# Three PSUM banks as three tiles, and as one tile only while the scores of two heads hold them

## The chip, the cores and the metric

The kernel runs on 1 core of one Trainium2 chip. The metric is device time in microseconds (us), the median of the runs. TensorE (PE) multiplies matrices; its products go to PSUM, which this kernel uses as eight banks of 128 partitions by 512 fp32 values, and VectorE (DVE) and ScalarE (ACT) read them there. GpSimd (POOL) does some of the work on SBUF, and SyncE (SP) issues the DMAs.

## The reference

An attention layer with a bias made by a small network, a feed-forward layer, and a layer of eight experts of which each token takes one. Cut to what matters:

```python
# attention: q, k, v are (2, 8, 576, 64)
scores = q @ k^T / sqrt(64) + bias        # bias: relu(x @ w1 + b1) @ w2, x from the positions
attn = exp(scores - max); attn /= sum(attn) + 1e-9
x = (attn @ v) as (1152, 512)
# feed-forward
h = x @ w_in                              # 512 -> 2048
g = h * tanh(log(1 + exp(h)))
x = g @ w_out                             # 2048 -> 512
# experts: each token to the expert of its largest logit, at most `capacity` tokens each
y = relu(x_e @ w1[e]) @ w2[e]
out[i] = gate[i] * y[expert of i, place of i]
```

## The kernel before, in words

The 1152 tokens are worked off in five tiles of rows (`NIT` = 4 tiles of 128 rows of both batches, and one of the rest). For each tile there are blocks of the bias (`bias_block`, L473 on PE, read out at L487 to L490), the attention (`pair` for the scores and the softmax, `recips`, `pv_pair`), the feed-forward layer (`mlp_a`, L726 on PE, read at L731 by ACT and at L283 by DVE; `mlp_b`, L759) and the choice of the expert (`y_out`, `rank_of`; L827, L843, L848, L907). Until about 460 us these parts are interleaved; after that the experts run one by one (L1182 to L1271).

Each of these steps is recorded with `op(...)`. The table `ORDER` says in which order the recorded steps are emitted and on which engine each runs. This order is fixed by hand ahead of the build, so each engine's queue is fixed, and an engine that waits at the head of its queue holds all that stands behind it. What an instruction waits for is not written in the kernel: the framework records, tile by tile, who wrote and read, and puts semaphore waits in front of an instruction that comes too soon.

PSUM is shared out by the ring `RB` of eight slots, one for a bank. Slots 3 to 7 (`pb0` to `pb4`) are five tiles of 512 columns. Slots 0 to 2 are slices of one tile, `ps`, of 3 x 512 columns:

```python
ps_ = psp.tile([P, 3, 512], F32, name="ps")
RB = Ring([ps_[:, i] for i in range(3)] + [psp.tile([P, 512], F32, name=f"pb{i}") for i in range(5)], {(0, 1, 2): ps_.rearrange("p a b -> p (a b)")})
```

`pair` takes the slots 0 to 2 together, since the scores of two heads fill 1536 columns: four products of 512 columns (L535; each counts twice in the trace, since fp32 goes in two passes) and a last piece (L538). DVE reads the two heads in turn (L552). At other times each of the three slots is taken alone, for a product of `mlp_a` (L726), a block of the bias (L473), three transposes (L561, copied to SBUF at L564), or small products (L599, L848, L907). `Ring.take` picks the free slot that was given back longest ago, and the three only when nothing else is free. The names `ps` and `pb` in the trace tell which tile an instruction writes or reads; which third of `ps` it is the trace does not tell.

Of the kernel before, what the change touches and what calls it, by code (L numbers as in the profile page):

```python
# [9 lines left out]
F32 = mybir.dt.float32  # L10
# [9 lines left out]
PSUM = bass.MemoryType.PSUM  # L20
DRAM = bass.MemoryType.DRAM

P = 128
# [119 lines left out]
class Buf:  # L143
    def __init__(self, ring, spans):
        self.ring, self.spans, self.left, self.slot = ring, spans, 0, None
# [6 lines left out]
class Ring:  # L152
# [12 lines left out]
    def take(self, b):  # L165
        def rank(x):
            whole = len(x) == 1 and any(x[0] in g and self.open(g) for g in self.groups)
            return whole, max(self.since[i] for i in x), x
        b.slot = min((x for x in b.spans if self.open(x)), key=rank)
        for i in b.slot:  # L170
            self.since[i] = None
# [4 lines left out]
            self.since[i] = self.clock  # L176


class Op:
    __slots__ = ("deps", "bufs", "allocs", "ways", "bytes", "late", "grp", "mode")  # L180


class Plan:
# [9 lines left out]
    def op(self, eng, ns, fn, r=(), w=(), p=(), bytes=0, alt=(), hold=(), lk=None, late=0.0, grp=None, mode=0):  # L193
        o = Op()
        o.ways = [(eng, ns, fn, eng == "POOL" if lk is None else bool(lk))] + [x if len(x) > 3 else x + (x[0] == "POOL",) for x in alt]
        o.late, o.bytes, o.grp, o.mode = late, bytes, grp, mode
        o.deps, o.bufs, o.allocs = set(), [], []
        for x in r:
            assert self.wr.get(x), ("read before any write", x)
            o.deps.update(self.wr[x])  # L200
            self.rd.setdefault(x, []).append(o)
        for x in list(w) + list(p):
            o.deps.update(self.rd.get(x, ()))
            if isinstance(x, Buf) and (x in p or not self.wr.get(x)):
                o.allocs.append(x)
        for x in w:
            o.deps.update(self.wr.get(x, ()))
            self.wr[x], self.rd[x] = [o], []
        for x in p:
            if self.rd.get(x):  # L210
                o.deps.update(self.wr.get(x, ()))
                self.wr[x], self.rd[x] = [o], []
            else:
                self.wr.setdefault(x, []).append(o)
        o.deps.discard(o)
        for x in {id(x): x for x in list(r) + list(w) + list(p) if isinstance(x, Buf)}.values():
            x.left += 1
            o.bufs.append(x)
        for x in hold:
            x.left += 1  # L220
            o.bufs.append(x)
        self.ops.append(o)
        return o
# [40 lines left out]
def tile_kernel(ctx: ExitStack, tc: tile.TileContext, a: dict, cap: int):  # L264
# [9 lines left out]
    def pool_of(stack, name, side="left", space=None):  # L274
        args = dict(name=name, bufs=1)
        args.update(dict(space=space) if space is not None else dict(side=side))
        return stack.enter_context(tc.tile_pool(**args))
# [35 lines left out]
    psp = pool_of(ph1, "psp", space=PSUM)  # L313
# [26 lines left out]
    def ring(p, name, n, shape, dt):  # L340
        return Ring([p.tile(shape, dt, name=f"{name}{i}") for i in range(n)])
# [9 lines left out]
    RX = Ring([PX[:, 2048 * i:2048 * i + 2048].rearrange("p (a b c) -> p a b c", a=2, b=4) for i in (1, 0)])  # L351
    RM = ring(p1, "rm", 12, [P, 2], F32)
    RSM = ring(p1, "rsm", 3, [P, 8], F32)
    ps_ = psp.tile([P, 3, 512], F32, name="ps")
    RB = Ring([ps_[:, i] for i in range(3)] + [psp.tile([P, 512], F32, name=f"pb{i}") for i in range(5)], {(0, 1, 2): ps_.rearrange("p a b -> p (a b)")})
    LONG = range(3, 8)


# [52 lines left out]
    def over_partitions(col, r):  # L411


        ps = pl.buf(RB)
        op("PE", 300, lambda: pe.matmul(ps.t[:, 0:P], col.to_broadcast([P, P]), ident, start=True, stop=True), bytes=0.5, r=r + ["ident"], w=[ps])
# [27 lines left out]
    def bias_const():  # L443
        cps = pl.buf(RB)

        def f():
            for c in range(4):
                pe.matmul(cps.t[32 * c:32 * c + 32, 0:1], w2s, b1c, start=True, stop=True)
        op("PE", 150, f, bytes=0.5, r=["w2s", "b1"], w=[cps], mode=3)
        op("ACT", c_act(1), lambda: act.copy(cb, cps.t[:, 0:1]), r=[cps], w=["cb"])  # L450
# [3 lines left out]
    def bias_block(blk):  # L454
# [12 lines left out]
        for d0 in range(0, dn, 512):  # L467
            d1 = min(dn, d0 + 512)
            ps = pl.buf(RB)

# [53 lines left out]
    def pair(it, ct, b):  # L524
        s_ = pl.buf(RB, group=True)
        q_ = qs[it]
# [29 lines left out]
        for n in range(3):  # L556
            pa = pl.buf(RB)

# [19 lines left out]
    def recips(it, ct):  # L578
        sm, n = sums[it, ct], 2 if it < NIT else 1

        rb[it, ct] = b_ = pl.buf(R2)
        rp = pl.buf(RB)
        wide = lambda: b_.t[:, 256:256 + P * n]
# [551 lines left out]
    man = tc.manual_schedule()  # L1135
    man.__enter__()
    pl.emit()
    ph1.close()


# [243 lines left out]
```

## Time and profile before

| what | value |
|---|---|
| time, median of 3 runs | 589.54 us (588.83 to 595.59) |
| the profiled execution's own time | 590.54 us |
| its span, first to last instruction | 588.8 us |
| busy on PE | 501.7 us (85%) |
| busy on DVE, ACT, POOL | 409.5, 355.5, 148.8 us |
| mean granted TensorE clock | 0.947 of full speed |

The span is counted from the first instruction to the last; the time of an execution has 1.7 us more around it. Busy time is an average over the whole span; a wait is read from the idle time of an engine just before an instruction, which the profile puts down to the instruction that ended last of those waited for.

### The profile page before, as it was taken

The page shows a single profiled execution, that of the slowest core. Times are in us where ns is not written, and L with a number is a line of the kernel's source. Part 1 is how long each engine was busy: PE and PEld are TensorE (multiplying, and loading weights), DVE is VectorE, ACT ScalarE, POOL GpSimd, SP SyncE. Part 2 cuts the span into 40 slices and gives each one's busy share as a digit, 9 for nine tenths or more (in the row PEclk, how much of TensorE's full clock was granted, in tenths as well). Part 3 has the DMA queues.
Part 4 walks back from the last instruction along what each step waited for, and adds up shares of the span by engine and source line. Part 5 has one row for each costly group of instructions (what it writes and reads, how often), then busy time and mean ns, then how long its engine had stood idle before and what let it go on. Part 6 is the DMA issues. An engine that isn't in the chain of part 4 may idle for free.

```text
span 588.8 us, 11288 instructions
## 1 busy us (share of the span) xinstructions
PE 501.7 (85%) x4212; PEld 353.1 (60%) x4212; DVE 409.5 (70%) x957; ACT 355.5 (60%) x718; POOL 148.8 (25%) x162
## 2 busy tenths in 40 slices
PE   1655788998979788999999999999899379999975
PEld 0211455675567453445578756689558369998963
DVE  5999999887856466786656774559878634746363
ACT  6999998775575586548864673326563134535351
POOL 3641424203102232301020432102523411131312
PEclk9876799999999998999999999999999669999998
DMA  7998866500102024242574000104105155181810
GB/s 295 382 344 265 294 226 195 204 1 1 41 1 89 15 81 124 80 143 77 178 203 150 0 1 3 38 1 164 72 2 180 19 189 178 51 303 60 299 42 29
DMA packets 28468, 73.92 MB, mean 126 GB/s; under 512 B 5126, under 2 KB 5254, under 8 KB 26352
## 3 DMA queue, kind: packets, MB, share of 16 engines
q1 hardware_dynamic: 26704, 68.95, 34.7%
q0 software_dynamic: 1696, 4.11, 2.2%
q8 instruction: 36, 0.59, 0.4%
q14 instruction: 32, 0.26, 0.2%
HBM read 55.67 MB, written 17.61 MB: 124 GB/s over the span
## 4 chain that ended last, share of the span: by engine, by line
PE 44%; DVE 22%; issue 15%; DMA 7%; ACT 7%; POOL 3%; SPq 0%; POOLq 0%; DVEq 0%; ACTq 0%
PE pb L759 9%; PE pb L726 8%; DMA xg<-yscr,gid 5%; PE ps L726 4%; PE ps L535 4%; PE pb L618 4%; DVE rw L283 4%; PE pb L561 3%; DVE ra L552 2%; DVE ra L280 2%; PE ps L561 2%; DVE WOt L283 2%; DMA w2b<-w 2%; PE ps L538 2%; PE pb L763 2%
## 5 line engine op out<-in xcount | busy, mean ns | idle before, releaser
L726 PEld LDWEIGHTS <-WIt 128*128 128x128 f16 x960 | 85.2, 98 | 25.9 <-issue 11.2
L726 PE MATMUL pb<-PX,WIt 128*128 128x256 f16 (+1 forms) x648 | 71.5, 265 | 2.7 <-DVE ra L283 2.0
L461 ACT ACTIVATE ra<-AT,b1c,stab 128x384 f32<-128x384 f32 (+13 forms) x74 | 51.8, 740 | 5.3 <-PE ps L473 2.2
L759 PE MATMUL pb<-WOt,ra 128*128 128x512 f16 x228 | 54.3, 383 | 0.2 <-POOL ra L741 0.2
L473 PE MATMUL pb<-ra,w2s 128*32 128x512 f32 (+15 forms) x246 | 39.5, 612 | 16.5 <-DVE rbe L490 5.3
L553 ACT ACTIVATE ra<-ra,rm 128x576 f32<-128x576 f32 x56 | 43.2, 774 | 10.2 <-DVE rm L552 9.9
L535 PE MATMUL ps<-AT,rq 64*128 64x512 f32 (+1 forms) x160 | 42.5, 662 | 8.0 <-DVE rm L552 6.6
L280 POOL TENSOR_SCALAR rw<-rw 128x1024 uint32<-128x1024 uint32 (+1 forms) x19 | 28.6, 1507 | 59.4 <-DMA rw<-wo 23.3
L552 DVE CUSTOM_DVE_ANT_0 ra<-ps,ra 128x576 f32<-128x576 f32 x50 | 36.4, 753 | 8.4 <-PE ps L538 3.9
L1215 PE MATMUL py<-HH,W 128*128 128x288 f32 x288 | 40.5, 298 | 0.0
L1014 DVE TENSOR_TENSOR W<-AT,W 128x1024 fp32r<-128x1024 f32 x28 | 33.7, 1224 | 9.6 <-ACT W L1013 8.9
L726 PE MATMUL ps<-PX,WIt 128*128 128x256 f16 (+1 forms) x312 | 31.7, 256 | 9.2 <-ACT ra L461 3.1
L1215 PEld LDWEIGHTS py<-HH,W 128*128 128x128 f32 x288 | 38.9, 188 | 0.0
L759 PE MATMUL pb<-WOt,rw 128*128 128x512 f16 x156 | 38.3, 387 | 0.0
L618 PE MATMUL pb<-ra,AT 128*64 128x128 f32 (+1 forms) x620 | 35.8, 266 | 0.9 <-DVE ra L632 0.9
L759 PEld LDWEIGHTS <-ra 128*128 128x128 f16 x228 | 21.8, 98 | 24.1 <-issue 1.5
L618 PEld LDWEIGHTS pb<-ra,AT 128*64 128x64 f32 x620 | 30.6, 137 | 5.1 <-issue 2.5
L283 DVE SCALAR_TENSOR_TENSOR rw<-rw 128x1024 int32<-128x1024 int32 (+1 forms) x26 | 31.8, 1226 | 0.1
L473 PEld LDWEIGHTS pb<-ra,w2s 128*32 128x32 f32 x246 | 10.1, 128 | 33.0 <-issue 8.6
L561 PE MATMUL pb<-ident,ra 128*128 128x128 f32 x180 | 28.6, 286 | 1.3 <-ACT ra L553 0.9
L1013 ACT ACTIVATE W<-AT 128x1024 fp32r<-128x1024 f32 x28 | 29.0, 1055 | 0.0
L538 PEld LDWEIGHTS ps<-AT,rq 128*128 128x128 f32 (+1 forms) x80 | 10.7, 183 | 29.0 <-issue 28.2
(395 smaller groups left out, 1101.5 us busy)
## 6 DMA issues: line engine op xcount, KB each, us to landing
AT<-m SPq DMA_DIRECT2D x32, 512.0 KB, 6.0
bscr<-rbe SPq DMA_DIRECT2D x36, 295.5 KB, 2.9
rw<-wo SPq DMA_DIRECT2D x8, 1024.0 KB, 5.0
ra<-bscr SPq DMA_DIRECT2D x28, 288.0 KB, 4.1
WOt<-wi SPq DMA_DIRECT2D x4, 1024.0 KB, 9.8
rw<-wi SPq DMA_DIRECT2D x4, 1024.0 KB, 9.1
AT<-k SPq DMA_DIRECT2D x4, 576.0 KB, 7.3
out<-ra SPq DMA_DIRECT2D x9, 256.0 KB, 6.0
```

Of the source, the lines that this page charges most:

```text
L280: eng.tensor_scalar(out=out, in0=in0, scalar1=s1, scalar2=s2, op0=op0, op1=op1)
L283: (eng or dve).scalar_tensor_tensor(out=out, in0=in0, scalar=s, in1=in1, op0=op0, op1=op1)
L461: on_act = lambda h_=h_, g=g: act.activation(h_.t[:, 0:dn], T[:, 0:dn], AF.Relu, scale=stab[:, g:g + 1], bias=b1c)
L473: pe.matmul(ps.t[32 * c:32 * c + 32, 0:d1 - d0], w2s, hs[c].t[:, d0:d1], start=True, stop=True)
L535: pe.matmul(s_.t[r, 1024 * i:1024 * i + 512], q_.t[hs, c], kraw[hs, k0 + 576 * bb:k0 + 576 * bb + 512], start=True, stop=True)
L552: op("DVE", c_dve(S), lambda i=i, own=own, m_=m_, b_=b_: dve.tensor_tensor_reduce(out=own(), in0=blk(s_.t[:, 960 * i:960 * i + S]), in1=bl ...
L553: op("ACT", c_act(S, 2), lambda i=i, m_=m_, col=col: act.activation(t_.t[:, S * i:S * i + S], t_.t[:, S * i:S * i + S], AF.Exp, bias=m_.t[ ...
L561: pe.transpose(pa.t[:, P * j:P * j + P], t_.t[:, 384 * n + P * j:384 * n + P * j + P], ident)
L618: pe.matmul(ov[64 * i:64 * i + 64, ct % 2, w * bb:w * bb + w], v_, t_.t[:, at + c0:at + c0 + w], start=n == 0, stop=n == 4)
L726: pe.matmul(ps.t[:, n * f_:n * f_ + n], WI[:, wv, ct, P * ft:P * ft + P], xt.t[:, xv, ct, 0:n], start=i == 0, stop=i == 11)
L759: pe.matmul(y_.t, gv()[:, g2, c:c + P], WO[:, wv, ft], **kw)
L1215: pe.matmul(ps[:, 0:SL], W2[:, wv, ft, P * dt:P * dt + P], HH[:, hv, ft], start=ft == 0 and i == 0, stop=ft == 7 and i == 2)
```

## The change

The ring `RB` becomes a `Banks`, which opens a pool of PSUM tiles for slots 0 to 2 whenever their use changes. While `pair` holds them, the pool has one tile of 1536 columns; while slots are taken singly it has three tiles of 512 columns. `take` closes the pool and opens the next when a slot below 3 is taken in the other manner than last time. `pb0` to `pb4` stay as they are. `ORDER`, the steps and the choice of slots are untouched.

```diff
+class Banks(Ring):
+
+
+    def __init__(self, tiles, get):
+        super().__init__([None] * 3 + tiles, {(0, 1, 2): None})
+        self.get, self.pool, self.whole, self.count = get, ExitStack(), None, 0
+
+    def take(self, b):
+        super().take(b)
+        if b.slot[0] < 3 and self.whole is not (len(b.slot) == 3):
+            self.pool.close()
+            self.whole, self.count = len(b.slot) == 3, self.count + 1
+            new = self.get(self.pool, f"pz{self.count}", 1 if self.whole else 3)
+            if self.whole:
+                self.groups[b.slot] = new[0]
+            else:
+                self.tiles[:3] = new
+
...
-    ps_ = psp.tile([P, 3, 512], F32, name="ps")
-    RB = Ring([ps_[:, i] for i in range(3)] + [psp.tile([P, 512], F32, name=f"pb{i}") for i in range(5)], {(0, 1, 2): ps_.rearrange("p a b -> p (a b)")})
+    RB = Banks([psp.tile([P, 512], F32, name=f"pb{i}") for i in range(5)], lambda st, name, n: [p.tile([P, 1536 // n], F32, name=f"ps{i}") for p in [pool_of(st, name, space=PSUM)] for i in range(n)])
...
     pl.emit()
+    RB.pool.close()
     ph1.close()
```

In the built program the five `pb` tiles lie in banks 0 to 4 and the shared three in banks 5 to 7 (before: `ps` in 0 to 2). The pool is opened 22 times, 11 times with one tile and 11 times with three. Every engine has the same instructions in the same order as before; lines from 461 on stand 18 lower in the changed file (L726 is L744 there). What differs is the names of the tiles and the waits. In the rows below, the word in brackets names the semaphore of the engine that an instruction waits for; the number behind a tile's name tells tiles apart.

The first place is on PE near 161 us: three transposes, a block of the bias and the first product of a step of `mlp_a`, which hold the three banks. `ps_140` is the one tile. Before:

```order
L561 MATMUL ps_140<-ident_82,ra4_115 128x128 [waits Activation_49]
L561 MATMUL ps_140<-ident_82,ra4_115 128x128 x2
L473 MATMUL ps_140<-ra1_112,w2s_94 32x320 [waits Activation_49]
L473 MATMUL ps_140<-ra0_111,w2s_94 32x320
L473 MATMUL ps_140<-ra6_117,w2s_94 32x320 x2
L726 LDWEIGHTS WIt_105
L726 MATMUL ps_140<-PX_107,WIt_105 128x256
```

The same place now:

```order
L579 MATMUL ps1_1395<-ident_82,ra4_115 128x128 [waits Activation_49]
L579 MATMUL ps1_1395<-ident_82,ra4_115 128x128 x2
L491 MATMUL ps2_1396<-ra1_112,w2s_94 32x320
L491 MATMUL ps2_1396<-ra0_111,w2s_94 32x320
L491 MATMUL ps2_1396<-ra6_117,w2s_94 32x320 x2
L744 LDWEIGHTS WIt_105
L744 MATMUL ps0_1394<-PX_107,WIt_105 128x256 [waits Activation_49]
```

The wait for ACT has gone from the block of the bias, and one for ACT stands four products later, ahead of the step of `mlp_a`, whose bank `ps0` ACT had read last.

The second place is on PE near 168 us: three transposes, the transposes of `recips` into a `pb` tile, and the next step of `mlp_a`. Before:

```order
L561 MATMUL ps_140<-ident_82,rw0_108 128x128 x3
L599 MATMUL pb0_141<-ident_82,ra9_120 128x128 [waits Activation_49]
L599 MATMUL pb0_141<-ident_82,ra9_120 128x128
L726 LDWEIGHTS WIt_105
L726 MATMUL ps_140<-PX_107,WIt_105 128x256 [waits Activation_49]
```

The same place now:

```order
L579 MATMUL ps2_1396<-ident_82,rw0_108 128x128 [waits Activation_49]
L579 MATMUL ps2_1396<-ident_82,rw0_108 128x128 x2
L617 MATMUL pb0_140<-ident_82,ra9_120 128x128 [waits Activation_49]
L617 MATMUL pb0_140<-ident_82,ra9_120 128x128
L744 LDWEIGHTS WIt_105
L744 MATMUL ps1_1395<-PX_107,WIt_105 128x256 [waits DVE_49]
```

The step of `mlp_a` waited for ACT, which had read the step before it out of another bank; now it waits for DVE, which copies the transposes out of this bank (`ps1`).

The third place is on PE near 200 us: the end of a block of the bias and the next step of `mlp_a`. Before:

```order
L473 MATMUL ps_140<-rw0_108,w2s_94 32x320
L473 MATMUL ps_140<-ra7_118,w2s_94 32x320 [waits DMAHW6_49]
L473 MATMUL ps_140<-rw1_109,w2s_94 32x320 [waits Activation_49]
L726 LDWEIGHTS WIt_105 [waits DVE_49]
L726 MATMUL ps_140<-PX_107,WIt_105 128x256 [waits Activation_49]
```

The same place now:

```order
L491 MATMUL ps1_1395<-rw0_108,w2s_94 32x320
L491 MATMUL ps1_1395<-ra7_118,w2s_94 32x320 [waits DMAHW6_49]
L491 MATMUL ps1_1395<-rw1_109,w2s_94 32x320 [waits Activation_49]
L744 LDWEIGHTS WIt_105
L744 MATMUL ps2_1396<-PX_107,WIt_105 128x256
```

The two waits ahead of the step of `mlp_a`, for DVE and for ACT, have gone, and none has come in their place.

## Rows read from the trace of the kernel before

**Rows 1.** The page's first part: each engine's busy time, share of the span, instructions.

```profile
PE 501.7 (85%) x4212; PEld 353.1 (60%) x4212; DVE 409.5 (70%) x957; ACT 355.5 (60%) x718; POOL 148.8 (25%) x162
```

**Rows 2.** Groups of PE, 160 to 440 us: busy, mean ns; idle before them, releasers.

```profile
L726 PE MATMUL pb<-PX,WIt 128*128 128x256 f16 (+1 forms) x511 | 55.2, 263 | 0.2 <-POOL PX L292 0.2
L726 PE MATMUL ps<-PX,WIt 128*128 128x256 f16 (+1 forms) x312 | 31.7, 256 | 9.2 <-ACT ra L461 3.1 <-DVE rw L283 2.0 <-ACT rw L731 1.7
...
L618 PE MATMUL pb<-rw,AT 128*64 128x128 f32 (+1 forms) x180 | 10.5, 265 | 0.6 <-DVE ra L632 0.6
...
L848 PE MATMUL ps<-sum,lg 128*128 128x8 f32 x2 | 0.4, 266 | 2.9 <-ACT rw L731 2.9
```

**Rows 3.** Timeline of PE: start, length, instructions; in brackets idle before, releaser.

```profile
161.62 0.74 PE L473 MATMUL ps<-ra,w2s 128*32 128x320 f32 x8 [0.57 <-ACT ra L564]
...
165.60 0.55 PE L561 MATMUL ps<-ident,rw 128*128 128x128 f32 x3 [1.17 <-ACT rbe L488]
...
169.69 0.93 PE L726 MATMUL ps<-PX,WIt 128*128 128x256 f16 x7 [1.68 <-ACT rw L731]
...
190.28 0.93 PE L726 MATMUL ps<-PX,WIt 128*128 128x256 f16 x7 [1.05 <-ACT rbe L487]
...
200.75 0.94 PE L726 MATMUL ps<-PX,WIt 128*128 128x256 f16 x7 [3.10 <-ACT ra L461]
...
213.72 1.03 PE L726 MATMUL ps<-PX,WIt 128*128 128x256 f16 x8 [0.55 <-ACT rbe L488]
...
222.35 0.39 PE L848 MATMUL ps<-sum,lg 128*128 128x8 f32 x2 [2.87 <-ACT rw L731]
...
246.39 0.58 PE L473 MATMUL ps<-ra,w2s 128*32 128x464 f32 x1 [0.72 <-DVE ra L564]
...
253.79 1.13 PE L535 MATMUL ps<-AT,rq 64*128 64x512 f32 x4 [1.31 <-ACT rbe L487]
...
348.32 0.52 PE L561 MATMUL ps<-ident,ra 128*128 128x128 f32 x3 [0.74 <-DVE ra L564]
...
372.28 0.33 PE L599 MATMUL ps<-ident,ra 128*128 128x128 f32 x1 [0.56 <-DVE ra L564]
...
385.15 0.93 PE L726 MATMUL ps<-PX,WIt 128*128 128x256 f16 x7 [0.82 <-ACT ra L731]
...
414.29 0.93 PE L726 MATMUL ps<-PX,WIt 128*128 128x256 f16 x7 [0.68 <-DVE rw L283]
...
426.02 0.96 PE L726 MATMUL ps<-PX,WIt 128*128 128x128 f16 x14 [1.30 <-DVE rw L283]
```

**Rows 4.** Timeline near the first three stalls and the seventh, of PE, ACT and DVE.

```profile
158.86 0.55 PE L561 MATMUL ps<-ident,ra 128*128 128x128 f32 x3
159.25 1.47 PE L726 MATMUL pb<-PX,WIt 128*128 128x256 f16 x12
160.56 0.49 PE L561 MATMUL ps<-ident,ra 128*128 128x128 f32 x3
...
161.08 0.48 ACT L564 COPY ra<-ps 128x384 f32<-128x384 f32 x1 [1.79 <-PE ps L561]
...
167.90 1.02 DVE L564 COPY rw<-ps 128x384 f32<-128x384 f32 x2 [2.41 <-PE ps L561]
...
218.91 0.27 ACT L846 COPY lg<-pb 128x128 f32<-128x128 f32 x1 [1.42 <-PE pb L843]
```

**Rows 5.** Busy time of each engine in two stretches, then granted clock, DMA share, GB/s.

```profile
220.00:222.30 2.30, 0.00 (x0) 0.00 (x0) 2.14 (x5) 2.30 (x6) 0.00 (x0) 1.00 0.00 0
222.30:225.00 2.70, 2.65 (x9) 1.14 (x10) 1.93 (x6) 0.75 (x3) 2.10 (x2) 0.65 0.63 231
```

**Rows 6.** Timeline of PE from 222 us: products of the same form.

```profile
222.60 2.23 PE L759 MATMUL pb<-WOt,ra 128*128 128x512 f16 x6
224.62 2.42 PE L759 MATMUL pb<-WOt,rw 128*128 128x512 f16 x6
...
227.84 1.46 PE L759 MATMUL pb<-WOt,ra 128*128 128x512 f16 x6
```

**Rows 7.** The page's costliest groups: DVE's read of one head's scores.

```profile
L552 DVE CUSTOM_DVE_ANT_0 ra<-ps,ra 128x576 f32<-128x576 f32 x50 | 36.4, 753 | 8.4 <-PE ps L538 3.9 <-issue 3.8 <-PE pb L618 0.6
```

## The prediction

> **What bounds the kernel now.** I read the busy times first. PE is busy for 501.7 of 588.8 us and no other engine for more than 70% [rows 1], so what shortens the kernel is work taken from PE or idle time taken out of its queue. The edit takes no product away; it can only act on waits. So I read, second, PE's groups by line for 160 to 440 us, where the three shared banks are most in use and all parts interleave. The reader is to see what stands behind the second bar, the idle time before a group. The steps of `mlp_a` that go to the five separate tiles (`pb`) have 0.2 us of it over 511 products; the 312 that go to the shared tile (`ps`) have 9.2 us. The largest other `pb` group has 0.6 us, while two small products into `ps` alone have 2.9 us [rows 2]. The same product, the same releasing engines, and yet the idle time lies with one tile.
>
> Third, I followed PE's timeline and noted each product into `ps` that came after more than half a microsecond of idle time. From 160 us on there are 14 [rows 3]. Their idle times are 0.57, 1.17, 1.68, 1.05, 3.10, 0.55, 2.87, 0.72, 1.31, 0.74, 0.56, 0.82, 0.68 and 1.30, which is 17.12 us. After each of them PE goes on at once, so that the end of the program hangs on them.
>
> **What kind of waits they are.** Take the first. Three transposes go into one third of `ps` and end at 159.41 (158.86 and 0.55). ACT is free, but its copy of them starts only at 161.08, when the next three transposes, which go to another third, have ended at 161.05 (160.56 and 0.49). Then PE's block of the bias, for the last third, waits for that copy to end at 161.56 [rows 3, 4]. Neither wait is for the data or for the bank; both follow from the three banks being one tile to whatever sets the waits. At 167.90 DVE shows the same: it had been idle for 2.41 us when its copy began, behind the last products into `ps` [rows 4]. The order of the two programs says that these waits are the ones that go: at the first place the block of the bias has lost its wait, at the third the step of `mlp_a` has lost both.
>
> [...]
>
> **The change, part by part.**
>
> *Waits that go outright.* Nine stalls wait for an instruction that read or wrote another third, or for something behind such an instruction, and what remains to be waited for ended before PE was free: 0.57, 1.05, 3.10, 0.55, 2.87, 0.72, 0.56, 0.82 and 1.30, together 11.54 us [rows 3]. For the one of 2.87 it can be read: the small product needs ACT's copy `lg`, which ended at 219.18 (218.91 and 0.27), while the wait was for a read of `ps` that ended just ahead of 222.35 [rows 3, 4].
>
> *Waits that stay, but for something that comes sooner.* Five products wait for a true reader of their own bank, and that reader was itself held by a false wait: 1.17, 1.68, 1.31, 0.74 and 0.68, together 5.58 us [rows 3]. The one of 1.68 is the second place in the order: the step of `mlp_a` will wait for DVE's two copies, which began at 167.90 after 2.41 us of idleness [rows 4]; begun when their transposes are done, they are out of PE's way. The scores at 253.79 (1.31) take all three banks and truly need the last block of the bias read out, but ACT came to that late for the same reason.
>
> What is late next? After a stall is gone PE runs on to the next product whose wait was satisfied before, so it meets the engines behind it at the same distances as now: ACT and DVE get their inputs earlier by the same amount, and at 60% and 70% busy [rows 1] they are not the queue that sets the pace. A wait that is satisfied just in time still costs the step from release to start: 161.56 to 161.62, 0.06 us [rows 3, 4]. I keep this for all 14: 17.12 − 14 × 0.06 = 16.3 us. Bounds: 11.54 − 9 × 0.06 = 11.0 us where only the nine go, and 17.1 where nothing is kept.
>
> [...]
>
> [...]
>
> *What is added.* The pool is opened 22 times. At an opening, the first product waits for all that used the three banks before, PE's own products among them. In the order some of these products wait for two engines where they waited for one. Nothing in the trace shows a wait of PE for itself; the nearest row is the step of 0.06 us for a wait that is just satisfied, so 22 × 0.06 = 1.3 us at most where such waits are long fulfilled, and 0 where they lie beside products still running. I take 0.6. The idle time that covers it is none: PE is the busy engine.
>
> [...]
>
> *What is not touched.* From 460 us on, the experts use other tiles and start from the end of what stands ahead of them, so they move forward as a whole.
>
> **The sum.** Against the profiled execution: 590.54 − 16.3 − 1.7 + 0.6 = 573.1 us. That execution was 1.0 us above the median of 589.54, so the median becomes 572.1 us.
>
> **The rivals.**
>
> *Only the outright waits go.* When PE is earlier, the true readers of each bank may not be: ACT and DVE have other work queued ahead (ACT's L461 fills its gaps), and then the five second-hand stalls stay and the clock may drop as before. 590.54 − 11.0 + 0.6 − 1.0 = 579.1 us, or 577.4 with the clock's 1.7. For it: ACT is the named releaser in nine of the 14. Against: its idle times beside them, as the 1.79 us ahead of the copy at 161.08 [rows 4], show that it was waiting too, not busy.
>
> *The stalls are a lack of banks, and nothing goes.* All eight banks are in use, and a product that finds none free must wait however the banks are named. The time would be 589.5 us. [...] Against it stand the 0.2 us of the `pb` groups, which share the same pressure [rows 2], and the waits that the order shows to have gone.
>
> *Openings cost more than the false waits.* At an opening, the new tiles can only be used when all readers of the old are done. Where a single bank was free after one head's read, it now waits for the second too, 0.75 us [rows 7]; at worst PE stands for both heads' reads, 1.5 us, at each of 22 openings. That is 33 us, and 590.54 − 16.3 + 33 − 1.0 = 606 us, slower by 2.8%. It decides from 18.0 / 22 = 0.82 us an opening. Against it: half of the openings are for the scores, which took all three banks before too, and in the other half the scores' readers are mostly long done, since slots 0 to 2 are taken singly only when nothing else is free.
>
> **How the numbers follow.** Forecast 0.75, only the outright waits 0.15, nothing goes 0.06, slower 0.04. The range reaches up to the first rival's 579.1 and, for the scatter of the runs shown (0.7 us from the median to the fastest), to 579.8; down to 590.54 − 17.1 − 1.7 − 0.8 − 1.0 = 569.9, where nothing is kept of the 14, openings cost nothing and the idle time before the two `pb` groups goes as well (0.2 and 0.6 [rows 2]), and 0.7 less, 569.2. Left out are the two last rivals and some of the ends. About 2%, 11.8 us, is what a measurement of this kernel tells from no change; the line is at 577.7. The forecast lies below it, and a third of the first rival: 0.80 faster, 0.17 within, 0.03 slower.
>
> **What the changed profile would show.** PE's idle time before products into `ps0` to `ps2` from 145 to 430 us falls from 17 to under 2 us, and the `pb` groups stay near 1. ACT's and DVE's copies of transposes start within 0.1 us of their own third transpose where they were idle. The granted clock stays at 1.00 through the twelve products of `mlp_b`. Each engine has the same busy time, PE about 1.7 us less. The first product after an opening shows little idle time. I am wrong if the idle time turns up before `pb` products, before DVE's or ACT's reads with PE as the releaser, or at the openings; or if the clock drops at new places.

## The result and the profile after

The changed kernel takes 567.91 us (median of 4, 566.76 to 570.29) against 591.93 us for the kernel before (median of 4, 588.83 to 595.59): a ratio of 0.960, 95% interval 0.952 to 0.967. The time is 1.3 us below the lower end of the range and 4.2 us below the forecast of 572.1. That forecast stood on a median before of 589.54 us, of three runs; a fourth run makes it 591.93. By the gain it is therefore further off: 17.4 us were forecast (589.54 − 572.1), and 24.0 were measured. The profiled execution took 566.76 us, with a span of 565.0; its counterpart before took 590.54, with 588.8. So 23.8 us of span are to be explained.

The first part of the page of the changed kernel answers to [rows 1]:

```profile
PE 496.1 (88%) x4212; PEld 351.2 (62%) x4212; DVE 410.1 (73%) x957; ACT 354.5 (63%) x718; POOL 148.7 (26%) x162
```

The same instructions, in the same order. PE's groups from 145 us to 425 us (the same work as in [rows 2], and a little more), with busy time, mean ns and idle time before them:

```profile
L744 PE MATMUL pb<-PX,WIt 128*128 128x256 f16 (+1 forms) x528 | 57.2, 263 | 0.2 <-POOL PX L311 0.2
...
L744 PE MATMUL ps<-PX,WIt 128*128 128x256 f16 (+1 forms) x312 | 31.7, 256 | 0.7 <-DVE rw L302 0.7
...
L866 PE MATMUL ps<-sum,lg 128*128 128x8 f32 x2 | 0.4, 266 | 0.0
```

The steps of `mlp_a` into the three banks have 0.7 us of idle time left of 9.2, the small product L848 (two instructions, now L866) none of 2.9, and nothing has moved to this `pb` group. PE's timeline at the first three of the places of [rows 3], with idle time in brackets where there is any:

```profile
156.82 0.52 PE L579 MATMUL ps<-ident,ra 128*128 128x128 f32 x3
157.18 1.47 PE L744 MATMUL pb<-PX,WIt 128*128 128x256 f16 x12
158.49 0.49 PE L579 MATMUL ps<-ident,ra 128*128 128x128 f32 x3
158.91 0.75 PE L491 MATMUL ps<-ra,w2s 128*32 128x320 f32 x8
159.59 1.48 PE L744 MATMUL ps<-PX,WIt 128*128 128x256 f16 x12
...
161.56 0.49 PE L579 MATMUL ps<-ident,rw 128*128 128x128 f32 x3
161.89 1.47 PE L744 MATMUL ps<-PX,WIt 128*128 128x256 f16 x12
163.20 0.49 PE L579 MATMUL ps<-ident,rw 128*128 128x128 f32 x3
163.53 0.38 PE L617 MATMUL pb<-ident,ra 128*128 128x128 f32 x2
163.75 1.47 PE L744 MATMUL ps<-PX,WIt 128*128 128x256 f16 x12
```

There is no bracket in these rows. More than that: the transposes ahead of the bias end at 158.98 (158.49 and 0.49), and the bias starts at 158.91. Without the wait, the bias starts 0.07 us before the product ahead of it has ended, by the ends that the profile gives (it models them). ACT's copy of the first transposes, in the timeline of ACT, no longer waits for the later ones:

```profile
157.38 0.48 ACT L582 COPY ra<-ps 128x384 f32<-128x384 f32 x1 [0.21 <-PE ps L579]
```

These transposes end at 157.34 (156.82 and 0.52), and the copy starts 0.04 us later; before, it started 1.67 us after the end of its transposes, 161.08 against 159.41 [rows 4]. At the seventh place, PE's timeline answers to [rows 6]:

```profile
208.51 0.39 PE L866 MATMUL ps<-sum,lg 128*128 128x8 f32 x2
208.75 1.46 PE L777 MATMUL pb<-WOt,ra 128*128 128x512 f16 x6
210.04 1.46 PE L777 MATMUL pb<-WOt,rw 128*128 128x512 f16 x6
```

The twelve products of `mlp_b` run at a granted clock of 1.00 (from 208.5 to 211.5 us): 1.46 us for six, as six of the same form take behind the drop in the kernel before [rows 6].

To see where the 23.8 us lie, I cut each span at the same two instructions: the block of the bias behind the first stall, and the last tile's transposes of `y_out` (L827, now L845), behind the last stall. Windows with PE's busy time first (its instructions in brackets), the granted clock third from the end. Before:

```profile
0.00:161.62 161.62, 117.09 (x841) 66.75 (x841) 145.51 (x292) 131.18 (x258) 52.67 (x70) 0.89 0.58 205
161.62:446.98 285.36, 267.21 (x2410) 176.65 (x2410) 186.91 (x483) 170.37 (x367) 65.12 (x62) 0.99 0.24 77
446.98:588.80 141.82, 117.39 (x963) 109.73 (x963) 77.04 (x184) 53.97 (x95) 30.97 (x30) 0.91 0.40 133
```

After:

```profile
0.00:158.91 158.91, 115.63 (x841) 65.71 (x841) 143.59 (x291) 132.42 (x261) 52.49 (x70) 0.89 0.59 208
158.91:425.43 266.52, 263.89 (x2410) 176.21 (x2410) 189.67 (x484) 168.19 (x364) 65.77 (x62) 1.00 0.26 82
425.43:565.00 139.57, 116.58 (x963) 109.24 (x963) 76.81 (x184) 53.93 (x95) 30.44 (x30) 0.92 0.40 135
```

PE's counts are the same in each stretch. The middle one, where the forecast placed everything, is 18.8 us shorter: PE's idle time fell from 18.2 (285.36 − 267.21) to 2.6, and its busy time by 3.3. The first stretch is 2.7 us shorter, of which 0.6 is the first stall; the last is 2.3 us shorter. The forecast had nothing for these two but that one stall.

### The profile page after: what moved, and what is told of

Read it like the earlier page. It is cut to its first block, busy times and chain, and to the rows that moved or that the text cites. A ratio compares the mean times of both kernels' runs of the same rounds, so it can differ in the third digit from the quotient of the medians.

```text
span 565.0 us, 11301 instructions
## 1 busy us (share of the span) xinstructions
PE 496.1 (88%) x4212; PEld 351.2 (62%) x4212; DVE 410.1 (73%) x957; ACT 354.5 (63%) x718; POOL 148.7 (26%) x162
## 4 chain that ended last, share of the span: by engine, by line
PE 43%; DVE 24%; issue 14%; DMA 9%; ACT 6%; POOL 3%; POOLq 0%; DVEq 0%; ACTq 0%; SPq 0%
PE pb L777 10%; PE pb L744 8%; DMA xg<-yscr,gid 5%; PE pb L636 5%; DVE rw L302 4%; PE ps L553 4%; PE ps L744 4%; DVE ra L570 3%; PE pb L579 3%; DVE ra L299 2%; DVE ra L302 2%; PE ps L579 2%; PE pb L491 2%; DMA tbl<-pk,rm 2%; PE ps L556 2%
## 5 line engine op out<-in xcount | busy, mean ns | idle before, releaser
L744 PEld LDWEIGHTS <-WIt 128*128 128x128 f16 x960 | 85.2, 98 | 15.6 <-issue 6.2
L744 PE MATMUL pb<-PX,WIt 128*128 128x256 f16 (+1 forms) x648 | 71.5, 265 | 1.6 <-DVE ra L302 0.9
L744 PE MATMUL ps<-PX,WIt 128*128 128x256 f16 (+1 forms) x312 | 31.7, 256 | 0.7 <-DVE rw L302 0.7
L299 DVE TENSOR_SCALAR ra<-AT,stab,nb 128x512 f32<-128x512 f32 (+10 forms) x47 | 26.9, 596 | 2.3 <-PE pb L491 2.1
```

Of the source, the lines that this page charges most:

```text
L299: eng.tensor_scalar(out=out, in0=in0, scalar1=s1, scalar2=s2, op0=op0, op1=op1)
L744: pe.matmul(ps.t[:, n * f_:n * f_ + n], WI[:, wv, ct, P * ft:P * ft + P], xt.t[:, xv, ct, 0:n], start=i == 0, stop=i == 11)
```

## The experiments

**Both kernels again.** No edit; each profiled anew.

> The kernel before, unchanged, for a second profile of it. The changed kernel reached the first of the 14 stalls about 2.1 us sooner than the kernel before, ahead of every wait that the forecast counted. Theory 1: this is scatter of the first 160 us, where the loads set the pace; then this profile has the block of the bias that follows the first stall somewhere between 159 and 164 us, not again at 161.6. Theory 2: it comes of the change; then it stands at 161.6 within 0.3 us. The 14 stalls before products into ps come again, 17.1 us in sum within 1 us, under both. Ratio 1.00.

> The changed kernel, unchanged, for a second profile of it. Theory 1: the block of the bias that follows the first stall stands somewhere between 156 and 162 us. Theory 2: at 158.9 within 0.3 us. From there to the end of the feed-forward layers PE needs the same time as in the first profile within 0.5 us, no stall of over 0.5 us before a product into the three tiles, no drop of the granted clock near the twelve products of mlp_b. Ratio 0.96.

Measured: 592.82 us, ratio 1.001 [0.998, 1.004], and 567.42 us, 0.959 [0.954, 0.964]. Before shows the 14 stalls once more, 17.12 us in sum. After shows none of the 14, but in both of its profiles there is one new wait of 0.70 us before a product into the three tiles, which the expectation had ruled out; the part on the prediction comes back to it. The block of the bias behind the first stall stands at 162.12 and 159.09 us. The changed kernel is ahead there once more, by 3.0 us, but this does not decide between the two theories: 159.09 is within the 0.3 us of theory 2, and 162.12 is not. The experiment on the fourth opening, below, finds where 1.5 us of the lead come from. The middle stretch is 286.38 and 266.56 us, so after repeats to 0.04 us there. The last stretch is 140.7 and 139.8, so that the tail's 2.3 us of the first pair is 0.9 in the second; over the profiles of this study in which the `pb` tiles are untouched it lies between 139.6 and 144.4 us, in no order that follows the edits. I take the tail for scatter. What differs between the two profiles of before is where the clock fell. PE's timeline of the repeat, at stall 5 and then at stall 7:

```profile
201.25 2.74 PE L726 MATMUL ps<-PX,WIt 128*128 128x256 f16 x12 [3.10 <-ACT ra L461]
203.79 4.29 PE L759 MATMUL pb<-WOt,ra 128*128 128x512 f16 x12
...
225.61 0.39 PE L848 MATMUL ps<-sum,lg 128*128 128x8 f32 x2 [2.87 <-ACT rw L731]
225.85 1.46 PE L759 MATMUL pb<-WOt,ra 128*128 128x512 f16 x6
227.14 1.46 PE L759 MATMUL pb<-WOt,rw 128*128 128x512 f16 x6
```

This time it is the stall of 3.10 us behind which the products are slow (2.74 for twelve that take 1.47 in the changed kernel, 4.29 for twelve that take 2.75; the granted clock is 0.51 from 200.0 to 203.5 us and 0.52 from there to 207.0), and the products behind the stall of 2.87 us take 1.46 us for six, as in the changed kernel. In the first profile it was the other way round [rows 5, 6]. Of the six profiles here of kernels with both stalls (these two and four below), the clock falls behind stall 5 in two, behind stall 7 in two, and behind both in two (in the kernel with the openings alone it is 0.50 from 197.9 to 201.3 us and 0.50 from 221.8 to 225.2); in none does it stay up.

**The openings without the three tiles.** The pool is opened and closed as in the changed kernel, but one tile is taken each time, and single products get slices of it. Against the changed kernel:

```diff
-            new = self.get(self.pool, f"pz{self.count}", 1 if self.whole else 3)
+            t = self.get(self.pool, f"pz{self.count}", 1)[0]
             if self.whole:
-                self.groups[b.slot] = new[0]
+                self.groups[b.slot] = t
             else:
-                self.tiles[:3] = new
+                self.tiles[:3] = [t[:, 512 * i:512 * i + 512] for i in range(3)]
```

> The pool is closed and opened 22 times as in the changed kernel, and its tiles lie in banks 5 to 7, but each opening gets one tile of 1536 columns, and single products go to slices of it. Theory (three banks in one tile are what makes the waits): the 14 stalls are all back, the time is that of the kernel before, ratio 0.995 to 1.005 plus at most 1.3 us for openings. Rival (the openings, or the other banks, bring the gain): ratio 0.96.

Measured: 589.22 us, 0.996 [0.993, 0.999]. The stalls are all there, 17.09 us. The group of PE, from 145 to 440 us, with the idle time of [rows 2]:

```profile
L744 PE MATMUL ps<-PX,WIt 128*128 128x256 f16 (+1 forms) x312 | 33.0, 262 | 9.2 <-ACT ra L479 3.1 <-DVE rw L302 2.0 <-ACT rw L749 1.7
```

So the gain is not from opening the pool, but from the tiles being three: 21.8 us from this kernel's 589.22 to 567.42. What is left between this kernel and the one before, 2.1 us, is taken up under "Left open".

**The shared tile in other banks.** The five `pb` tiles are taken first in the kernel before, so that the shared tile lies in the last three banks.

```diff
+    pb_ = [psp.tile([P, 512], F32, name=f"pb{i}") for i in range(5)]
     ps_ = psp.tile([P, 3, 512], F32, name="ps")
-    RB = Ring([ps_[:, i] for i in range(3)] + [psp.tile([P, 512], F32, name=f"pb{i}") for i in range(5)], {(0, 1, 2): ps_.rearrange("p a b -> p (a b)")})
+    RB = Ring([ps_[:, i] for i in range(3)] + pb_, {(0, 1, 2): ps_.rearrange("p a b -> p (a b)")})
```

> The kernel before with the five tiles laid out first, so that the one shared tile lies in banks 5 to 7 as in the changed kernel. Theory: which banks they are changes nothing, ratio 0.995 to 1.005, the 14 stalls stand as before. Rival (the place in PSUM matters): ratio below 0.99.

Measured: 593.29 us, 1.002 [0.999, 1.005]; the 14 stalls sum to 17.11 us. Where the banks lie makes no difference that these runs can tell.

**Three tiles at one opening, and at all but this one.** Stalls 1 to 7 of the 14 lie within the eighth opening. In the first kernel only this opening takes three tiles, in the second all others do; the rest get slices of one tile.

```diff
-            new = self.get(self.pool, f"pz{self.count}", 1 if self.whole else 3)
+            split = not self.whole and self.count == 8
+            new = self.get(self.pool, f"pz{self.count}", 3 if split else 1)
             if self.whole:
                 self.groups[b.slot] = new[0]
-            else:
+            elif split:
                 self.tiles[:3] = new
+            else:
+                self.tiles[:3] = [new[0][:, 512 * i:512 * i + 512] for i in range(3)]
```

The second has `self.count != 8` there.

> Three tiles only at the eighth opening, which holds all single products from 158 to 236 us (stalls 1 to 7 of the 14, 10.99 us of idle time); at the ten other openings for single products one tile with slices. If each stall is worth its idle time and a little more (0.1 us each, since the product then overlaps the one before it) and the clock keeps up at the twelve products of mlp_b (1.7 us): 10.99 + 0.7 + 1.7 = 13.4 us less than before, ratio 0.977. If the stalls hang together (a wait that goes here is met again at the ones left): 7 us or less, ratio above 0.988.

> The other part alone: three tiles at ten openings, one tile with slices at the eighth (158 to 236 us). Stalls 8 to 14 go, 6.13 us of idle time: 6.13 + 0.7 = 6.8 us less than before, ratio 0.988; the seven stalls and the drop of the clock of the eighth opening stand. With the other part this makes 20.2 us; if the whole change brings more than the sum of the two, the rest is not in these waits.

Measured: 577.81 us, 0.977 [0.972, 0.983], and 581.98 us, 0.982 [0.976, 0.988]. In the first, stalls 1 to 7 are gone and the other seven are left, 6.12 us; in the second it is the reverse, with 10.99 us, and the new wait of 0.7 us is there too. Against 591.02 us for before in these runs the two gains are 13.2 and 9.0 us, 22.2 together, and by the middle stretch 12.7 and 6.0 us, 18.7 of the whole edit's 18.8 (285.36 less 272.63 and 279.34). By the medians that is 1.8 short of the whole change's 24.0, which is within their intervals. The second gain, for which 6.8 us were expected, is 2.2 more by the medians and 0.8 less by the middle stretch. The two halves add up, so the stalls of one half are not met again in the other.

**One stall put back.** In the changed kernel, one small product (two instructions) is put in front of stall 7's, into the same part of the same bank, which the true product then overwrites. It reads what ACT writes when it reads the neighbouring bank, the instruction that stall 7 waited for.

```diff
-    gg, yy = {}, {}
+    gg, yy, us = {}, {}, {}
...
+        us[len(pl.ops)] = u_
...
-        op("PE", 140, lambda: pe.matmul(pg.t[:, 0:E], lt.t, sum4, start=True, stop=True), r=[lt, "sum4"], w=[pg])
+
+        def f():
+            if 2 * it + b == 1:
+                pe.matmul(pg.t[:, 0:E], us[808].t[:, 0:P], sum4, start=True, stop=True)
+            pe.matmul(pg.t[:, 0:E], lt.t, sum4, start=True, stop=True)
+        op("PE", 140, f, r=[lt, "sum4"], w=[pg])
```

> The changed kernel with one wait put back: ahead of the small product L848 (stall 7, 2.87 us before the change) stands a small product of the same form that reads what ACT had written last there, and which the true product then overwrites, so PE waits for that ACT instruction as it did before. The product itself costs about 0.25 us. If the idle time brings down the clock: a stall of 2.3 to 3.0 us at about 208.5 us, the twelve products of mlp_b behind it take 1.5 to 2 us longer than 2.9 us, and the time is 4 to 5 us above the changed kernel. If the drop of the clock was chance: 2.5 to 3.2 us above, the twelve products at 2.9 us.

Measured: 573.97 us, 0.970 [0.965, 0.975], 6.6 us more than the changed kernel's 567.42, where 4 to 5 were expected; the middle stretch is 6.15 us longer. PE's timeline:

```profile
211.28 0.60 PE L870 MATMUL ps<-sum,rw 128*128 128x8 f32 x2 [2.87 <-ACT rw L750]
211.73 0.57 PE L871 MATMUL ps<-sum,lg 128*128 128x8 f32 x2
212.16 2.72 PE L778 MATMUL pb<-WOt,ra 128*128 128x512 f16 x6
214.67 2.77 PE L778 MATMUL pb<-WOt,rw 128*128 128x512 f16 x6
```

The windows around it, PE's busy time first, the granted clock third from the end:

```profile
208.50:211.30 2.80, 0.02 (x1) 0.02 (x1) 2.25 (x5) 2.80 (x7) 1.07 (x1) 0.88 0.00 0
211.30:214.00 2.70, 2.70 (x9) 1.57 (x10) 1.55 (x4) 0.45 (x1) 2.18 (x2) 0.50 0.63 231
214.00:217.00 3.00, 3.00 (x9) 0.91 (x6) 0.85 (x3) 0.72 (x1) 0.09 (x1) 0.50 0.00 0
```

The stall of 2.87 us is back, to the hundredth. The granted clock is 0.50 behind it, and the twelve products take 5.49 us in place of 2.92 (1.46 twice), 2.6 us more, where 1.5 to 2 were expected. With everything else as in the changed kernel, the stall costs its own length and 3.3 us behind it (6.15 − 2.87): 2.6 of these are the twelve products at the lower clock, and 0.45 is the product that was added (211.28 to 211.73, where the true one starts).

**Stall 5 put back.** The same with a small product ahead of the step of `mlp_a` at stall 5, which reads the ends of a block of the bias.

```diff
+    bes = {}
...
+                bes[len(pl.ops)] = be
...
-            def f(f_=f_):
+            def f(f_=f_, own=len(pl.ops)):
                 ft = 2 * fp + f_
+                if own == 807:
+                    pe.matmul(ps.t[:, n:n + E], bes[910].t[:, 0:P], sum4, start=True, stop=True)
```

> The changed kernel with the wait of stall 5 (3.10 us) put back: ahead of that step of mlp_a stands a small product that reads what DVE's last read of the bias block wrote, overwritten by the true product. The first profile before showed no drop of the clock behind this stall, a second profile of the same kernel did. If a stall of this length brings the clock down in some executions: a stall near 3 us, and a drop within 3 us of it in this profile or not, the time 3.2 us above the changed kernel without, 5 to 6.5 with it. If the drop hangs on the work and not on the stall: 3.2 us above, no drop.

Measured: 570.03 us, 0.964 [0.957, 0.971]. PE's timeline at this place:

```profile
190.35 0.39 PE L745 MATMUL ps<-sum,rbe 128*128 128x8 f32 x2 [1.37 <-DVE rbe L509]
190.59 1.47 PE L748 MATMUL ps<-PX,WIt 128*128 128x256 f16 x12
```

The window there, the granted clock third from the end:

```profile
190.00:193.00 3.00, 2.65 (x20) 1.92 (x21) 2.34 (x5) 2.85 (x6) 0.00 (x0) 1.00 0.00 0
```

The wait is only 1.37 us long, since the instruction it waits for, DVE's last read of the block, comes sooner when the other false waits are gone; the middle stretch is 1.66 us longer. What a stall of 3.1 us alone does to the clock, this run does not tell. It does tell that 1.7 of the 3.10 us (3.10 − 1.37) were inherited from other false waits.

**Twice the openings.** The pool is opened anew whenever all three banks are free, 48 times in place of 22.

```diff
+        free = all(self.since[i] is not None for i in range(3))
         super().take(b)
-        if b.slot[0] < 3 and self.whole is not (len(b.slot) == 3):
+        if b.slot[0] < 3 and (free or self.whole is not (len(b.slot) == 3)):
```

> The changed kernel with the pool closed and opened also whenever a single product finds all three slots free, 48 openings in place of 22. If an opening costs 0.06 us: 1.6 us more, ratio to before 0.962. If it costs nothing: as the changed kernel, 0.960 within 0.003. If it holds PE for DVE's reads (0.75 us or more): 20 us more, ratio 0.995.

Measured: 569.86 us, 0.962 [0.957, 0.967]. The middle stretch is 266.80 us, 0.28 more than after, so there an opening costs PE next to nothing. Most of the 2.4 us is the tail (142.9 us), which I take for scatter. But at one place of the first stretch PE waits where it does not in the changed kernel:

```profile
127.22 0.49 PE L434 MATMUL ps<-ident,gl 128*128 128x128 f32 x2 [0.17 <-ACT ra L583]
```

The added openings are the only edit, so one of the new tiles is held here until ACT has read the old ones. What such a short wait is worth at this place, the next experiment shows.

**Three tiles at the fourth opening alone, and at all but this one.** The first stretch is shorter by 2.7 us, and 1.5 of them lie at 126 to 136 us: from three transposes to a step of `mlp_a` behind them it is 8.7 us before and 7.2 after. Before, with the timeline of PE, POOL and DVE there (rows in order of their start):

```profile
126.99 0.49 PE L561 MATMUL ps<-ident,ra 128*128 128x128 f32 x3
...
129.18 0.49 PE L415 MATMUL ps<-ident,gl 128*128 128x128 f32 x2 [0.17 <-ACT ra L564]
...
131.62 1.46 POOL L736 TENSOR_TENSOR ra<-ra,ra 128x512 f32<-128x512 f32 x1 [14.41 <-ACT ra L735]
...
131.87 1.76 DVE L736 TENSOR_TENSOR ra<-ra,ra 128x512 f32<-128x512 f32 x1
...
135.68 1.47 PE L726 MATMUL pb<-PX,WIt 128*128 128x256 f16 x12 [1.98 <-DVE ra L283]
```

After:

```profile
126.37 0.49 PE L579 MATMUL ps<-ident,ra 128*128 128x128 f32 x3
...
128.23 0.39 PE L433 MATMUL ps<-ident,gl 128*128 128x128 f32 x2
...
130.81 0.69 DVE L754 TENSOR_TENSOR ra<-ra,ra 128x512 f32<-128x512 f32 x1
...
131.00 2.85 POOL L754 TENSOR_TENSOR ra<-ra,ra 128x512 f32<-128x512 f32 x2 [14.42 <-ACT ra L753]
...
133.56 1.47 PE L744 MATMUL pb<-PX,WIt 128*128 128x256 f16 x12 [0.91 <-DVE ra L302]
```

Before, a false wait of 0.17 us holds two transposes of the gate's sums, and DVE's chain behind them. DVE then comes to its L736 0.25 us after POOL has begun an instruction of the same line, and takes 1.76 us. After, DVE is 0.19 us ahead of POOL and takes 0.69. (The two instructions of POOL that are merged in the last row but one take 1.63 and 1.27 us.) The theory: the 0.17 us decide which of the two is first, and by that 1.5 us; the rival: it is scatter. The kernels are those of the eighth opening with 4 for 8.

> The reverse: three tiles at the fourth opening alone, one tile with slices at the ten others. Theory: 7.2 us from the transposes to the step of mlp_a, and all 14 stalls after 158 us as in the kernel before, 17.1 us; ratio 0.993 to 0.998. Rival: 8.7 us.

> The changed kernel with one tile and slices at the fourth opening alone (the single products at 126 to 130 us). The profiles so far have there a wait of 0.17 us before the product L433 in every kernel that waits for ACT's copy out of another third, and with it a DVE instruction of 1.76 us in place of 0.69, which started 0.25 us after a POOL instruction in place of 0.19 us before it. Theory (the short wait decides which of the two goes first, and that costs 1.07 us): from the transposes at 126 us to the step of mlp_a at 134 us 8.7 us in place of 7.2, the rest as in the changed kernel, no stall of over 0.5 us before a product into ps later on; ratio 0.962. Rival (chance of the run): 7.2 us.

Measured: 588.98 us, 0.995 [0.991, 0.999], and 568.73 us, 0.962 [0.955, 0.969]. The timeline of DVE decides. Of the first kernel:

```profile
129.92 0.69 DVE L757 TENSOR_TENSOR ra<-ra,ra 128x512 f32<-128x512 f32 x1
```

Of the second:

```profile
130.01 1.76 DVE L757 TENSOR_TENSOR ra<-ra,ra 128x512 f32<-128x512 f32 x1
```

With three tiles at this opening alone, the place takes 7.2 us, and all 14 later stalls are there (17.10 us); with one tile there alone, the wait of 0.17 us is back and the place takes 8.7 us, while the middle stretch is as in the changed kernel. It is not scatter: in each of the 13 profiles of this study in which the `pb` tiles are untouched the place takes 8.7 us where the wait of 0.17 us is there, and 7.2 where it is not.

Of the two engines the rows show this: DVE's 1.76 us end 0.55 us after POOL's 1.46 do (133.63 against 133.08), and ahead of POOL it takes 0.69. Behind DVE, POOL's instruction takes 1.63 us, only 0.17 more than the 1.46 that it takes when it is first. Why DVE takes longer behind POOL, no run shows.

**Two other banks made one tile.** If a shared tile is the cause, it must make the same waits elsewhere. In the changed kernel two of the five `pb` banks become one tile, `pt`.

```diff
+    pt2 = psp.tile([P, 2, 512], F32, name="pt2")
-    RB = Banks([psp.tile([P, 512], F32, name=f"pb{i}") for i in range(5)], lambda ...
+    RB = Banks([psp.tile([P, 512], F32, name=f"pb{i}") for i in range(3)] + [pt2[:, i] for i in range(2)], lambda ...
```

> The changed kernel with two of the five other banks (pb3 and pb4) as slices of one tile of 1024 columns. Theory (any banks in one tile wait for each other): new idle time on PE before products into this tile, 3 to 15 us in sum, and as much more time, ratio 0.965 to 0.985. Rival (the waits belong to the tile of the scores, which changes between whole and single use): ratio 0.960 within 0.003.

Measured: 610.50 us, 1.034 [1.024, 1.043], 43 us more than the changed kernel and slower than the kernel before. Groups of PE, from 145 to 465 us:

```profile
L745 PE MATMUL pb<-PX,WIt 128*128 128x256 f16 (+1 forms) x336 | 36.4, 261 | 0.0
L745 PE MATMUL ps<-PX,WIt 128*128 128x256 f16 (+1 forms) x312 | 32.9, 262 | 0.0
L778 PE MATMUL pt<-WOt,ra 128*128 128x512 f16 x126 | 29.8, 379 | 7.0 <-DVE rw L760 3.7 <-ACT rbe L507 2.0 <-ACT ra L750 0.8
...
L745 PE MATMUL pt<-PX,WIt 128*128 128x256 f16 (+1 forms) x204 | 23.4, 266 | 4.1 <-DVE rr L299 1.8 <-ACT rw L750 1.3 <-ACT ra L583 0.6
```

The same step of `mlp_a` has no idle time at `ps` and `pb`, and 4.1 us at `pt`. On the page, PE's busy time is 505.0 us of a span of 605.8: 100.8 us idle against 68.9 after, and 8.9 us more busy at a mean granted clock of 0.935 against 0.949. The mechanism is as expected, its price far above the 3 to 15 us. The likely reason is that these two banks hold sums that are kept over many products, so that a neighbour waits longer; no run tests this by itself.

## Why the prediction was right in kind and short in size

**What bounds, and what kind of waits.** Right. The idle time lay with one tile, and it went with the tile: the openings alone leave all 14 stalls, other banks leave them, the two halves of the edit add up, and a new shared tile has stalls of its own. All five stalls that the text called second hand went, with the nine it called outright; of those nine, stall 5 was partly second hand too (1.37 of 3.10 us came back with its reader). What held the readers was the same cause, so the distinction carried no risk.

**"I keep this for all 14: 17.12 − 14 × 0.06 = 16.3".** The step that was mis-sized, and of the wrong sign. The 0.06 us is what the product at 161.62 us needed from its release to its start [rows 3, 4]. Of the 14 only one is late by a little (the 0.56 at 372.28, of which 0.09 is left, for a true reader of its bank); the others are released early, and then a product starts before the last one's end, by 0.07 us at the first place (158.98 against 158.91) and by 0.07 to 0.16 at twelve others, 1.5 us net. The term is 17.1 + 1.5 = 18.6 us, in place of 16.3. This does not hang on the modelled ends: counted from the start of the product ahead to the start of the product itself, the 14 places are 18.6 us shorter together. So the 17.1 "where nothing is kept" was no bound either, and the lower end of the range, which was built on it, stood too high.

**The clock, 1.7 us.** The term is an estimate from [rows 5, 6]: 4.65 us for the twelve products where the granted clock averages 0.65 (222.3 to 225.0 us), less 2.92 at 1.46 us for six, with the stall of 2.87 us taken as the cause. The profiled pair bears it out: PE's busy time in the middle stretch falls by 3.3 us, of which 1.7 are the twelve products; the rest is in the main the overlap just named. But one execution was read as if all were like it. The repeat has the drop at stall 5, where it costs 2.8 us by these rows (2.74 − 1.47 and 4.29 − 2.75), and the kernel with the openings alone has one at each. Of the six profiles with both stalls four have one drop and two have two, and six without the two (after, its repeat, and the kernels with twice the openings, with three tiles at the eighth opening alone, with one tile at the fourth, and with the 1.37 us at stall 5) have none from 160 to 425 us, where their granted clock is 1.00. The drops cost 1.7, 2.7, 3.0, 3.4, 1.7 and 1.7 us in these six, 2.4 in the mean, so for the median the term is some 2.4 us in place of 1.7. For both stalls 1.7 us each would make 3.4, which came in one of the six only. Behind the stall of 2.87 us that was put back the granted clock was 0.50; but in a single execution it may fall behind one stall and not behind the other.

**The openings, 0.6 us.** Too dear. 26 openings more cost 0.28 us in the middle stretch, some 0.01 us each; at that rate 22 cost about 0.2. The rival needed 0.82 us an opening to decide, some 75 times as much. That holds where the readers of the old tiles are done; at 127 us in the kernel with twice the openings they were not, and an opening brought back 0.17 us of waiting.

**"From 160 us on there are 14".** The search for stalls began at 160 us and at half a microsecond. These limits left out the 0.17 us at 129 us, worth 1.5 us since it decides between DVE and POOL. No bound of the sum reached there.

**What the sum lacked on the other side.** PE, being sooner, meets two new waits, both for DVE, at `mlp_b` and at `mlp_a`. In PE's timeline of the changed kernel:

```profile
397.89 3.01 PE L777 MATMUL pb<-WOt,ra 128*128 128x512 f16 x12 [0.56 <-DVE ra L302]
...
405.53 1.67 PE L744 MATMUL ps<-PX,WIt 128*128 128x128 f16 x27 [0.70 <-DVE rw L302]
```

With their lost overlap they cost 1.5 us. The prediction's "it meets the engines behind it at the same distances as now" failed there. So for the profiled pair: 18.6 for the stalls, 1.7 for the clock and 1.5 for the place at 129 us, less 1.5 for the new waits, is 20.3 us by named causes, of 23.8; 2.3 are the tail. Of the 1.2 that are left, 0.8 lie in the middle stretch: the products of the block of the bias behind stall 8 follow each other faster, by 0.4 us in all, and two waits near its end, too short to be counted among the 14, are shorter by 0.4. The rest, about 0.5 in the first stretch, I can't place.

**The rivals.** Only the outright waits go: no, all went. Lack of banks: no; eight banks are eight banks before and after, and the stalls went. Openings: as above.

**The marks named ahead.** Idle time before products into `ps` fell to about 1.1 us (under 2 was said), ACT's copies start 0.04 us behind their transposes and DVE's 0.11 (0.1 was said), the clock stays at 1.00 through the middle, and the first product after an opening waits for 0.2 us at most in the middle stretch. One sign of being wrong did show: idle time before `pb` products from 145 to 430 us rose from 1.0 to 1.5 us, by the new wait of 0.56. PE's busy time fell by 5.6 us and not 1.7: 3.3 in the middle as above, and the rest in the first and last stretch, where the granted clock differs from profile to profile (0.86 to 0.90 in the first and 0.91 to 0.92 in the last, over two profiles of each kernel).

**The range.** Its lower end counted each term at its nearest edge, with 17.1 us for the stalls, and allowed 0.7 us for scatter, while the runs of before span 588.83 to 595.59. In the profiled pair the gain is 23.8 us against 17.4 in the sum, 6.4 more: 2.3 are the overlap (18.6 for 16.3), 1.5 the place at 129 us, 0.6 the openings (of which no more than some 0.2 came), 2.3 the tail and 1.2 the small rest; the new waits take 1.5 back. The tail is scatter, and that it added 2.3 us here was chance (0.9 in the second pair); but the repeat's median, 567.42 us, lies below the range too, so the miss as a whole is not.

**Left open.** Why the kernel with the openings alone is 2.1 us below before (interval 0.7 to 4.0), with its stalls all in place; its first stretch is 159.5 us long against 161.6 and 162.1. Whether a stall of 3 us alone brings the clock down each time: with the stall of 2.87 us it fell in five profiles of seven, with that of 3.10 in four of six.

## What to carry to other kernels

Give every bank that is used for itself a tile for itself, and a tile over several only for the time in which one instruction reads them all: what set the waits here went by tiles (9.2 us of idle time at the shared tile and 0.2 at the five others, for the same product [rows 2]), and the shared one tied together engines that had nothing to do with each other. To find such waits, group the bounding engine's idle time by the tile it writes; the same product with idle time at one tile and none at another is the sign. When summing them up, count the overlap that a stall prevents (here 1.5 us for 14 stalls), the clock behind it (some 2.4 us) and the short waits upstream (0.17 us, worth 1.5), and look at more than one execution.

## What was not expected of the hardware

The sum of the stalls repeats to 0.03 us between executions (17.12, 17.12, 17.09, 17.11 and 17.10 us in the five profiles that have all 14), while the granted clock behind the same stall does not: 2.87 us of idle time were followed by products that took 1.46 us for six in one profile and in another by products that took 2.72 and 2.77 us for six, at a granted clock of 0.50. An instruction of DVE on 128x512 elements took 0.69 us when it began 0.19 us ahead of one of POOL, and 1.76 us when it began 0.25 us behind it, so that 0.17 us of waiting cost 1.5 us. And the last stretch took from 139.6 to 144.4 us in kernels with the same work there.
